# A three-stage float64 decode (two ReLUs and four VectorE operations) becomes a two-stage one (one parametric ReLU and two VectorE operations)

## The chip, the cores and the metric

The kernel runs on one core of one Trainium2 chip. The metric is device time in microseconds (us): median of 3 runs 1004.88 us (1004.45 to 1008.42). Five engines of the core work side by side, each through its own list of instructions in order: PE (TensorE: matmuls, with its weight loads PEld), DVE (VectorE), ACT (ScalarE), POOL (GpSimd) and SP (SyncE, which here issues every DMA). An instruction that waits for another engine holds up all that stands behind it in its own list.

## The reference

A linear attention with a decaying state (4 batches, 8 heads, 768 positions, head size 48), then two feed-forward layers over 3072 tokens of width 384:

```
cur   = outer(u * k_t, v_t)                      # per batch and head, 48 x 48
y_t   = r_t @ (state + cur)
state = w[:, None] * state + outer(k_t, v_t)
x = y as (batch, position, head * 48)
x = (sigmoid(x @ w_gate) * (x @ w_val)) @ w_out  # hidden width 1536
h = maximum(x @ w_in, 0)                         # hidden width 2048
out = (h * h) @ w_out2
```

The weights of both layers reach the device as 8-byte floats (their bytes are declared as int64); all products are float32 products.

## The kernel before, in words

The sequence is cut into 6 chunks of 128 positions; with 4 batches a chunk holds 512 tokens. An attention *unit* is one chunk of one batch (all eight heads). The hidden width of a layer is cut into blocks `f` of 128 columns (12 in layer 1, 16 in layer 2).

Every float32 matmul is made of three fp32r matmuls: both operands are split into a high and a low part, and high x high, low x high and high x low are added up in PSUM (`product`, `proj_out`). So one block `f` of layer 1 on 512 tokens is 9 matmuls for the gate (`pg`), 9 for the value (`pv`) and 9 for the output (`po`/`two`), each 128x128 by 128x512.

The work runs in *phases*. Phase 0 is layer 1 of chunk 0, blocks 0 to 6 only (`CUT` = 7); phases 1 to 5 are layer 1 of chunks 1 to 5, 12 blocks each; then chunk 0's other 5 blocks (`REDO`), and then layer 2 of all chunks. Ahead of phase 0 stands a start stretch with the four attention units of chunk 0. Beside the matmuls of phase `i` runs the attention of chunk `i + 1`: `unit_ops` spreads its steps over the phase's slots, three slots for each block, called by `fill(f, 0)`, `fill(f, 1)` and `fill(f, 2)` inside `inner`. There is no scheduler: the order of the code is the order on each engine.

A step `f` of layer 1 goes so: PE makes `pg`; ACT takes the sigmoid `s`; `fill(f, 0)`, which may hold a unit's matmuls into `ya` and `yb` (`attn_out`) and ACT's copies of them to `ys`; PE makes `pv` in the same PSUM buffer as `yb`, so after ACT's copy; DVE multiplies `pv` and `s`; ACT rounds the product to `gh`; `fill(f, 1)`; the rest `gl` = `s` - `gh` (on POOL in phase 0, on DVE later); PE adds the output product of the block before (`finish`); `fill(f, 2)`.

The weights lie in HBM in 68 *raw* pieces of 128 x 384 eight-byte numbers: for layer 1 gate, value and output of each block, so that block `f` needs pieces 3f, 3f+1 and 3f+2. Each piece is decoded once, by `convert()`, and stays in SBUF in two float32 parts, `wu`. The slots call `convert()`, at most once each (twice in the first slot of phase 0): about three pieces a block in phase 0, 15 pieces over phase 1, the 32 pieces of layer 2 during phase 5 and `REDO`.

The `n`-th call of `convert()` works on several pieces at once, in stages:

- piece n: two ReLUs on ACT (L146, L147) turn the low word into min(low / 2^29, 7), three bits
- piece n-1: DVE puts together the sign bit of the high word and those three bits in `wt_` (L159), and clears the sign in the top 16 bits (L167)
- piece n-2: DVE subtracts 16 * 896 from the top 16 bits and clamps at zero (L153), and puts the high word, shifted left by 3, into `wt_` (L163), which now holds float32
- piece n-3: ACT rounds `wt_` into the high part of `wu` (L132), POOL makes the low part (L133)

Four buffers hold raw pieces (`NRB`). Call `n` loads piece n+2, into the buffer of piece n-2, so SP waits for L163 there. Attention touches DVE too: `attn_mask` (L284, from PSUM), `attn_prep` (L232), `attn_sum` (L238, which gives `dv`), `attn_state` (L352, L353); ACT makes the diagonals `am` from `dv` (L248).

Of the kernel before, what the change touches and what calls it, by code (L numbers as in the profile page):

```python
# [7 lines left out]
F32 = mybir.dt.float32  # L8
F32R = mybir.dt.float32r
BF16 = mybir.dt.bfloat16  # L10
U8 = mybir.dt.uint8
I32 = mybir.dt.int32
U32 = mybir.dt.uint32
U16 = mybir.dt.uint16
I64 = mybir.dt.int64
AF = mybir.ActivationFunctionType
ALU = mybir.AluOpType
# [6 lines left out]
P = 128  # L24
DM = H * D
KT = DM // P
F1 = 12
# [14 lines left out]
def tile_kernel(  # L42
# [12 lines left out]
    nc = tc.nc  # L55
# [4 lines left out]
    sp = ctx.enter_context(tc.tile_pool(name="sp", bufs=2))  # L60
# [3 lines left out]
    NRB = 4  # L64
    NW = 36
    IN_W = 8
    CUT = 7
# [5 lines left out]
    seven = cp.tile([P, 1], F32, name="seven")  # L73
# [17 lines left out]
    def load_unit(n):  # L91

        if n >= NU:
            return
        c, b = units[n]
        got, o = [], 0
        for i, (tag, m, nb) in enumerate(PIECES):

            t = first[n][i] if n < IN_W else sp.tile([P, m], F32, tag=tag, name=tag, bufs=nb)
            got.append((t, rkv[c, b, :, o : o + m]))  # L100
            o += m
        for i in (2, 3, 0, 1):
            nc.sync.dma_start(out=got[i][0], in_=got[i][1])
        k_t[n], r_t[n] = (t[0:DP].rearrange("p (j t) -> p j t", j=HP) for t, _ in got[:2])
        kv_t[n], rn_t[n] = got[2][0], got[3][0]

    wunit = {}

    wqueue = [(w1[i, j], (1, i, j)) for i in range(F1) for j in range(3)]
    wqueue += [(w2[i, j], (2, i, j)) for i in range(F2) for j in range(2)]  # L110
    raws, parts, loaded = {}, {}, set()
    wn = [0]
    NWQ = len(wqueue)

    def load_raw(n):
        if n < NWQ and n not in loaded:
            loaded.add(n)
            raws[n] = sp.tile([P, KT * P], I64, tag="raw", name="raw", bufs=NRB)
            nc.sync.dma_start(out=raws[n], in_=wqueue[n][0])

    def convert():

        V = nc.vector
        n = wn[0]
        wn[0] += 1
        if n - 3 in parts:
            f1 = parts.pop(n - 3).bitcast(F32)  # L130
            w = wp.tile([P, 2, KT * P], F32R, tag="w", name="wu", bufs=NW)
            nc.scalar.copy(w[:, 0], f1)  # L132
            nc.gpsimd.tensor_tensor(out=w[:, 1], in0=f1, in1=w[:, 0].bitcast(F32), op=ALU.subtract)  # L133
            wunit[wqueue[n - 3][1]] = w

        def views(raw):
            two = [
                raw.bitcast(d).rearrange("p (n two) -> p n two", two=2) for d in (I32, F32, U32)
            ]
            top = raw.bitcast(U16).rearrange("p (n four) -> p n four", four=4)[:, :, 3]  # L140
            return [x[:, :, 0] for x in two] + [two[0][:, :, 1], top]

        if n < NWQ:

            lo, lof, lou, _, _ = views(raws[n])
            nc.scalar.activation(lof, lou, AF.Relu, bias=seven, scale=-(2.0**-29))  # L146
            nc.scalar.activation(lo, lof, AF.Relu, bias=seven, scale=-1.0)  # L147
        old, new = n - 2 in parts, 0 <= n - 1 < NWQ
        if old:

            raw, t = raws.pop(n - 2), parts[n - 2]
            _, _, _, hi, top = views(raw)
            V.tensor_scalar(  # L153
                out=top, in0=top, scalar1=16.0 * 896, scalar2=0.0, op0=ALU.subtract, op1=ALU.max
            )
        if new:
            lo, _, _, hi1, top1 = views(raws[n - 1])
            t1 = parts[n - 1] = sp.tile([P, KT * P], I32, tag="wt", name="wt_", bufs=3)
            V.scalar_tensor_tensor(  # L159
                out=t1, in0=hi1, scalar=-0x80000000, in1=lo, op0=ALU.bitwise_and, op1=ALU.bitwise_or  # L160
            )
        if old:
            V.scalar_tensor_tensor(  # L163
                out=t, in0=hi, scalar=3, in1=t, op0=ALU.logical_shift_left, op1=ALU.bitwise_or
            )
        if new:
            V.tensor_scalar(out=top1, in0=top1, scalar1=0x7FFF, scalar2=None, op0=ALU.bitwise_and)  # L167
        load_raw(n + NRB - 2)


    def tables():
# [49 lines left out]
    def attn_pre(n):  # L221
        if n >= NU:
            return
        rn = rn_t[n]
        side(n).tensor_tensor(out=rn, in0=rn, in1=kv_t[n][:, HD:], op=ALU.mult)
        side(n).tensor_tensor(out=rn, in0=rn, in1=u_bc, op=ALU.mult)

    def attn_prep(n):
        if n >= NU:
            return  # L230
        for t in (k_t[n], r_t[n]):
            nc.vector.tensor_mul(t, t, trk)  # L232

    def attn_sum(n):
        if n >= NU:
            return
        dv_t[n] = sp.tile([C, H], F32, tag="dv", name="dv", bufs=3)
        nc.vector.tensor_reduce(  # L238
            out=dv_t[n], in_=rn_t[n].rearrange("p (h d) -> p h d", d=D), axis=AX.X, op=ALU.add
        )  # L240
# [9 lines left out]
    def attn_kh(n):  # L250

        if n >= NU or units[n][0] == NCH - 1:
            return
        k = kv_t[n][:, HD:]
        side(n).tensor_tensor(out=k, in0=k, in1=th, op=ALU.mult)
# [285 lines left out]
    def warm(n):  # L541

        pw = pp.tile([P, T], F32, tag="g", name="pw") if n else None
        for _ in range(n):
            nc.tensor.matmul(pw, lhsT=idle[:, 0:P], rhs=idle, start=True, stop=True)

    with tc.manual_schedule():
        nc.vector.memset(idle, 0.0)
        warm(WARM0)
        nc.vector.memset(seven, 7.0)  # L550
        nc.scalar.activation(seven, seven, AF.Sigmoid)
        nc.vector.memset(seven, 7.0)
        nc.sync.dma_start(out=w_sb, in_=wt)
        id_sb = sp.tile([DP, D], F32, tag="ev", name="id_sb", bufs=2)
        maskf = sp.tile([C, C], F32, tag="ev", name="maskf", bufs=2)
        load_unit(0)
        nc.sync.dma_start(out=u_bc, in_=u.to_broadcast([C, H * D]))
        nc.sync.dma_start(out=anti, in_=antid)
        nc.sync.dma_start(out=maskf, in_=mask)
        nc.sync.dma_start(out=id_sb, in_=ident)  # L560
        load_unit(1)
        load_raw(0)
        load_raw(1)
        for n in range(2, B):
            load_unit(n)
            load_raw(n)
        powers = tables()
        attn_pre(0)
        nc.gpsimd.tensor_copy(mask8, maskf)
        attn_prep(0)  # L570
        attn_sum(0)
        attn_pre(1)
        attn_diag(0, 0)
        attn_diag(0, 1)
        attn_scores(0)
        attn_prep(1)
        attn_sum(1)
        state_tables(*powers)
        attn_mask(0)
        attn_diag(1, 0)  # L580
        attn_diag(1, 1)
        attn_kh(0)
        attn_kh(1)
        convert()
        for n in range(B):
            attn_scores(n + 1)
            attn_pre(n + 2)
            attn_prep(n + 2)
            warm(WARM_OUT[n])
            attn_out(n)  # L590
            attn_sum(n + 2)
            attn_mask(n + 1)
            attn_diag(n + 2, 0)
            attn_diag(n + 2, 1)
            attn_kh(n + 2)
            if n == 0:
                convert()
        for _ in range(2):
            convert()
        warm(WARM_X)  # L600
        for k in range(KT):
            x_from(0, k)
        for i, (layer, c, f0, f1) in enumerate(phases):
            ops = unit_ops(i + 1, f1 - f0) if i + 1 < NCH else []
            slot = 0

            def fill(f, j):

                nonlocal slot
                for op in ops[slot] if ops else []:  # L610
                    op()
                slot += 1
                lim = 0
                if i == 0:
                    lim = 3 * CUT + 3
                elif i == 1:
                    base = 3 * CUT + 3
                    lim = min(base + slot * (3 * F1 + 3 - base) // 27, 3 * F1 + 3)
                elif i == NCH - 1 and j < 2:
                    lim = min(3 * F1 + 3 * f - 1, 3 * F1 + 3 * CUT + 2)  # L620
                elif i == REDO and j < 2:
                    lim = 3 * F1 + 3 * f - 1
                elif i == REDO + 1 and j == 2:
                    lim = NWQ + 3
                for _ in range(2 if i == 0 and slot == 1 else 1):
                    if wn[0] < lim:
                        convert()

            for f in range(f0, f1):
                while (layer, f, 1) not in wunit:  # L630
                    convert()
                inner(i, f, fill)
        finish()
# [68 lines left out]
```

## Time and profile before

| | |
|---|---|
| median of 3 runs | 1004.88 us (1004.45 to 1008.42) |
| profiled execution, its own time | 1005.36 us |
| its span, first to last instruction | 1003.6 us (1.8 us lie around it) |
| mean granted TensorE clock | 0.985 of full |
| PE busy | 959.5 us, 96% |
| DVE busy | 544.6 us, 54% |
| ACT busy | 424.0 us, 42% |
| POOL busy | 133.9 us, 13% |

Busy shares are means over stretches that differ: after 216 us PE hardly rests and the others are half idle or more, in the first 220 us it is not so. A busy PE is also not PE at full speed: a matmul at the lower of the two clock levels is busy for twice as long. For the start, then, one goes stretch by stretch.

### The profile page before, as it was taken

The page shows a single profiled execution, that of the slowest core. Times are in us where ns is not written, and L with a number is a line of the kernel's source. Part 1 is how long each engine was busy: PE and PEld are TensorE (multiplying, and loading weights), DVE is VectorE, ACT ScalarE, POOL GpSimd, SP SyncE. Part 2 cuts the span into 40 slices and gives each one's busy share as a digit, 9 for nine tenths or more (in the row PEclk, how much of TensorE's full clock was granted, in tenths as well). Part 3 has the DMA queues.
Part 4 walks back from the last instruction along what each step waited for, and adds up shares of the span by engine and source line. Part 5 has one row for each costly group of instructions (what it writes and reads, how often), then busy time and mean ns, then how long its engine had stood idle before and what let it go on. Part 6 is the DMA issues. An engine that isn't in the chain of part 4 may idle for free.

```text
span 1003.6 us, 14066 instructions
## 1 busy us (share of the span) xinstructions
PE 959.5 (96%) x5544; PEld 760.7 (76%) x5544; DVE 544.6 (54%) x855; ACT 424.0 (42%) x870; POOL 133.9 (13%) x119
## 2 busy tenths in 40 slices
PE   7867798999999999999999999999999999999998
PEld 4555576778888888787888877888888888888886
DVE  7999978864444434431389787343433433433333
ACT  5766655643233323322377574232332322323322
POOL 6455643200000000000033132000000000000000
PEclk8989799999999999999999999999999999999999
DMA  9753544434122112200144440010010100100000
GB/s 316 245 179 101 154 130 129 131 106 132 52 60 73 61 52 59 89 7 15 63 125 124 160 148 27 1 63 0 1 64 1 47 17 1 63 1 1 32 1 31
DMA packets 42225, 76.75 MB, mean 76 GB/s; under 512 B 4912, under 2 KB 17584, under 8 KB 42160
## 3 DMA queue, kind: packets, MB, share of 16 engines
q1 hardware_dynamic: 42160, 75.87, 23.9%
q8 instruction: 43, 0.70, 0.3%
q14 instruction: 22, 0.18, 0.1%
HBM read 60.12 MB, written 11.01 MB: 71 GB/s over the span
## 4 chain that ended last, share of the span: by engine, by line
PE 80%; DVE 12%; DMA 3%; ACT 3%; issue 2%; SPq 1%; DVEq 0%; ACTq 0%
PE pg L384 31%; PE po L403 17%; PE two L403 14%; PE pv L384 12%; DVE raw L167 2%; DVE raw L153 2%; PE ya L298 2%; PE yb L298 1%; PE pa L266 1%; DVE am L284 1%; DMA raw<-in_w 1%; DVE first L232 1%; ACT am L248 1%; DVE s L527 1%; DMA first<-in_rkv 1%
## 5 line engine op out<-in xcount | busy, mean ns | idle before, releaser
L384 PE MATMUL pg<-xh,wu 128*128 128x512 f32 x1008 | 317.7, 400 | 11.7 <-ACT wu L132 7.5
L384 PEld LDWEIGHTS pg<-xh,wu 128*128 128x128 f32 x1008 | 191.2, 190 | 61.1 <-ACT wu L132 8.8
L531 ACT CAST gh<-s 128x512 fp32r<-128x512 f32 (+1 forms) x169 | 104.5, 618 | 219.4 <-DVE s L527 139.4
L384 PE MATMUL pg<-xl,wu 128*128 128x512 f32 x504 | 196.2, 397 | 0.0
L403 PE MATMUL po<-gh,wu 128*128 128x512 f32 (+1 forms) x542 | 169.0, 393 | 0.1
L530 DVE TENSOR_TENSOR s<-s 128x512 f32<-128x512 f32 (+1 forms) x97 | 66.7, 688 | 176.3 <-ACT s L529 176.3
L367 DVE TENSOR_TENSOR gl<-s,gh 128x512 fp32r<-128x512 f32 x162 | 113.1, 698 | 86.3 <-PE po L403 53.6
L384 PE MATMUL pv<-xh,wu 128*128 128x512 f32 x432 | 141.2, 408 | 15.8 <-ACT ys L336 11.3
L403 PE MATMUL two<-gh,wu 128*128 128x512 f32 x472 | 148.5, 395 | 0.0
L529 ACT ACTIVATE s<-pg 128x512 f32<-128x512 f32 (+1 forms) x97 | 57.5, 593 | 185.3 <-PE pg L384 185.3
L527 DVE TENSOR_TENSOR s<-pv,s 128x512 f32<-128x512 f32 x72 | 49.9, 692 | 150.4 <-PE pv L384 148.5
L403 PEld LDWEIGHTS po<-gh,wu 128*128 128x128 f32 x542 | 101.4, 188 | 24.6 <-ACT x2s L491 0.5
L384 PEld LDWEIGHTS pg<-xl,wu 128*128 128x128 f32 x504 | 95.6, 190 | 23.0 <-DVE xl L367 0.4
L384 PEld LDWEIGHTS pv<-xh,wu 128*128 128x128 f32 x432 | 80.4, 190 | 39.8 <-ACT ys L336 14.5
L403 PE MATMUL po<-gl,wu 128*128 128x512 f32 (+1 forms) x271 | 106.5, 393 | 1.3 <-DVE gl L367 1.3
L403 PEld LDWEIGHTS two<-gh,wu 128*128 128x128 f32 x472 | 89.3, 190 | 21.3
L403 PE MATMUL two<-gl,wu 128*128 128x512 f32 x236 | 93.0, 394 | 1.8 <-DVE gl L367 1.8
L384 PE MATMUL pv<-xl,wu 128*128 128x512 f32 x216 | 86.1, 399 | 0.0
L513 ACT ACTIVATE s<-pg 128x512 f32<-128x512 f32 x72 | 42.8, 595 | 101.8 <-PE pg L384 101.7
L248 ACT ACTIVATE am<-anti,dv 128x128 f32<-128x128 f32 x192 | 60.5, 391 | 19.7 <-DVE dv L238 19.7
L403 PEld LDWEIGHTS po<-gl,wu 128*128 128x128 f32 x271 | 50.8, 187 | 13.5 <-DVE gl L367 2.3
L167 DVE TENSOR_SCALAR raw<-raw 128x384 uint16<-128x384 uint16 x68 | 55.5, 816 | 0.0
(366 smaller groups left out, 967.0 us busy)
## 6 DMA issues: line engine op xcount, KB each, us to landing
raw<-in_w SPq DMA_DIRECT2D x68, 384.0 KB, 3.1
kv<-in_rkv SPq DMA_DIRECT2D x16, 384.0 KB, 3.2
xin<-x2d SPq DMA_DIRECT2D x6, 768.0 KB, 4.3
out<-x2s SPq DMA_DIRECT2D x18, 256.0 KB, 2.0
first<-in_rkv SPq DMA_DIRECT2D x16, 256.0 KB, 5.7
kT<-in_rkv SPq DMA_DIRECT2D x16, 256.0 KB, 4.7
rT<-in_rkv SPq DMA_DIRECT2D x16, 256.0 KB, 5.1
x2d<-x2s SPq DMA_DIRECT2D x15, 256.0 KB, 2.0
```

Source lines behind the costliest of these rows:

```text
L153: V.tensor_scalar(out=top, in0=top, scalar1=16.0 * 896, scalar2=0.0, op0=ALU.subtract, op1=ALU.max)
L167: V.tensor_scalar(out=top1, in0=top1, scalar1=0x7FFF, scalar2=None, op0=ALU.bitwise_and)
L248: nc.scalar.mul(am_t[n][:, h], anti, dv_t[n][:, h : h + 1])
L298: nc.tensor.matmul(out[64 * q : 64 * q + m], lhsT=lhsT, rhs=rhs, start=(bk, q) not in opened, stop=True, skip_group_check=True,)
L367: (eng or nc.vector).tensor_tensor(out=dst, in0=src, in1=high.bitcast(F32), op=ALU.subtract)
L384: nc.tensor.matmul(ps, lhsT=a, rhs=b_, start=(i == 0), stop=(i == len(pairs) - 1))
L403: nc.tensor.matmul(po[k][:, ts], lhsT=a, rhs=b_[:, ts], start=(first and m == 0), stop=(last and m == 2 and ts is cuts[-1]),)
L513: nc.scalar.activation(s, pg, AF.Sigmoid)
L527: nc.vector.tensor_tensor(out=s[:, ts], in0=pv[:, ts], in1=s[:, ts], op=ALU.mult)
L529: nc.scalar.activation(s[:, ts], pg[:, ts], AF.Relu)
L530: nc.vector.tensor_mul(s[:, ts], s[:, ts], s[:, ts])
L531: nc.scalar.copy(gh[:, ts], s[:, ts])
```

## The change

The three pieces of arithmetic are arranged anew. The top 16 bits of an eight-byte number are sign, 11 bits of exponent and 4 of mantissa; read as bfloat16 (sign, 8 and 7 bits) their exponent field holds the upper 8 bits of the long exponent. One parametric ReLU on ACT multiplies this bfloat16 by 2^-112 where it is positive, and by 2^-112 * 2^32 where it is negative: that rebases the exponent, and sets for a negative number the bit that the shift by 3 then brings to the sign's place. The three low bits come from one DVE operation (multiply, min), and one more DVE operation shifts and joins. Stages per call: piece n: ACT's parametric ReLU and DVE's low bits; piece n-1: DVE's shift and join; piece n-2: ACT's rounding and POOL's rest. The whole is one call shorter, and the bounds of the slots (`lim`) are lowered by one. Call `n` loads piece n+3, into the buffer of piece n-1.

```
@@ convert()
-        if n - 3 in parts:
-            f1 = parts.pop(n - 3).bitcast(F32)
+        if n - 2 in parts:
+            f1 = parts.pop(n - 2).bitcast(F32)
             w = wp.tile([P, 2, KT * P], F32R, tag="w", name="wu", bufs=NW)
             nc.scalar.copy(w[:, 0], f1)
             nc.gpsimd.tensor_tensor(out=w[:, 1], in0=f1, in1=w[:, 0].bitcast(F32), op=ALU.subtract)
...
+            top = raw.bitcast(BF16).rearrange("p (n four) -> p n four", four=4)[:, :, 3]
...
+        if n - 1 in raws:
+            lo, _, hi, _ = views(raws.pop(n - 1))
+            t = parts[n - 1] = sp.tile([P, KT * P], I32, tag="wt", name="wt_", bufs=3)
+            V.scalar_tensor_tensor(
+                out=t, in0=hi, scalar=3, in1=lo, op0=ALU.logical_shift_left, op1=ALU.bitwise_or
+            )
         if n < NWQ:
-            lo, lof, lou, _, _ = views(raws[n])
-            nc.scalar.activation(lof, lou, AF.Relu, bias=seven, scale=-(2.0**-29))
-            nc.scalar.activation(lo, lof, AF.Relu, bias=seven, scale=-1.0)
-        old, new = n - 2 in parts, 0 <= n - 1 < NWQ
-        if old:
-            raw, t = raws.pop(n - 2), parts[n - 2]
-            _, _, _, hi, top = views(raw)
+            lo, lou, _, top = views(raws[n])
+            nc.scalar.activation(top, top, AF.Prelu, scale=2.0**-112, alpha=2.0**32)
             V.tensor_scalar(
-                out=top, in0=top, scalar1=16.0 * 896, scalar2=0.0, op0=ALU.subtract, op1=ALU.max
+                out=lo, in0=lou, scalar1=2.0**-29, scalar2=7.0, op0=ALU.mult, op1=ALU.min
             )
-        if new:
-            lo, _, _, hi1, top1 = views(raws[n - 1])
-            t1 = parts[n - 1] = sp.tile([P, KT * P], I32, tag="wt", name="wt_", bufs=3)
-            V.scalar_tensor_tensor(
-                out=t1, in0=hi1, scalar=-0x80000000, in1=lo, op0=ALU.bitwise_and, op1=ALU.bitwise_or
-            )
-        if old:
-            V.scalar_tensor_tensor(
-                out=t, in0=hi, scalar=3, in1=t, op0=ALU.logical_shift_left, op1=ALU.bitwise_or
-            )
-        if new:
-            V.tensor_scalar(out=top1, in0=top1, scalar1=0x7FFF, scalar2=None, op0=ALU.bitwise_and)
-        load_raw(n + NRB - 2)
+        load_raw(n + NRB - 1)
@@ slots: 3 * CUT + 3 becomes 3 * CUT + 2, and so on
```

The first place is DVE in block 0 of phase 0, from the state update to the product `s`; `raw` and `wt_` belong to the decode. Before:

```order
L353 TENSOR_TENSOR state<-state,us 112x192
L153 TENSOR_SCALAR raw<-raw 128x384
L159 SCALAR_TENSOR_TENSOR wt__693<-raw 128x384
L163 SCALAR_TENSOR_TENSOR wt__604<-raw,wt__604 128x384
L167 TENSOR_SCALAR raw<-raw 128x384
L153 TENSOR_SCALAR raw<-raw 128x384
L159 SCALAR_TENSOR_TENSOR wt__705<-raw 128x384
L163 SCALAR_TENSOR_TENSOR wt__693<-raw,wt__693 128x384
L167 TENSOR_SCALAR raw<-raw 128x384
L527 TENSOR_TENSOR s<-pv,s 128x512
```

The same place on DVE now (line numbers are those of the changed kernel, 10 lower outside the decode):

```order
L343 TENSOR_TENSOR state<-state,us 112x192
L145 SCALAR_TENSOR_TENSOR wt__675<-raw 128x384
L155 TENSOR_SCALAR raw<-raw 128x384
L145 SCALAR_TENSOR_TENSOR wt__684<-raw 128x384
L155 TENSOR_SCALAR raw<-raw 128x384
L517 TENSOR_TENSOR s<-pv,s 128x512
```

Eight decode operations stood between the state update and `s`; four stand there now, and the join (L145) comes ahead of the low bits (L155).

The second place is ACT from block 0 to block 1 of phase 0, after `gh`: the diagonals `am`, the decode, the sigmoid, and the copies `us` and `ys` out of `yb` and `ya`. Before:

```order
L248 ACTIVATE am<-anti,dv 128x128 x4
L132 CAST wu<-wt__693 128x384
L146 ACTIVATE raw<-raw,seven 128x384
L147 ACTIVATE raw<-raw,seven 128x384
L248 ACTIVATE am<-anti,dv 128x128 x4
L132 CAST wu<-wt__705 128x384
L146 ACTIVATE raw<-raw,seven 128x384
L147 ACTIVATE raw<-raw,seven 128x384
L513 ACTIVATE s<-pg 128x512
L334 COPY us<-yb 112x192
L336 COPY ys<-yb 112x2x128
L337 COPY ys<-ya 112x2x128
```

The same place on ACT now:

```order
L238 ACTIVATE am<-anti,dv 128x128 x4
L132 CAST wu<-wt__684 128x384
L153 ACTIVATE raw<-raw 128x384
L238 ACTIVATE am<-anti,dv 128x128 x4
L132 CAST wu<-wt__716 128x384
L153 ACTIVATE raw<-raw 128x384
L503 ACTIVATE s<-pg 128x512
L324 COPY us<-yb 112x192
L326 COPY ys<-yb 112x2x128
L327 COPY ys<-ya 112x2x128
```

One ACTIVATE stands where two stood; the diagonals, the sigmoid and the copies keep their places.

The third place is SP's queue in the start stretch, at the first unit's `xr` transfers. Before:

```order
L339 DMA xr<-ys 48x3x128
L340 DMA xr<-ys 48x3x128
L103 DMA first<-in_rkv 128x768
L103 DMA first<-in_rkv 128x384
L103 DMA first<-in_rkv 128x512 x2
```

The same place in SP's queue now:

```order
L329 DMA xr<-ys 48x3x128
L330 DMA xr<-ys 48x3x128
L119 DMA raw<-in_w 128x384
L103 DMA first<-in_rkv 128x768
L103 DMA first<-in_rkv 128x384
L103 DMA first<-in_rkv 128x512 x2
```

The load of raw piece 4 moved from after the start stretch to ahead of the attention inputs of the sixth unit. It is the only load whose place in the queue changed; PE's and POOL's orders are as before.

## Rows read from the trace of the kernel before

**Rows 1.** The page: chain that ended last, share of the span by engine

```profile
PE 80%; DVE 12%; DMA 3%; ACT 3%; issue 2%; SPq 1%; DVEq 0%; ACTq 0%
```

**Rows 2.** Windows: busy time of PE, PEld, DVE, ACT, POOL; granted clock, DMA share, GB/s

```profile
0.00:40.00 40.00, 30.03 (x359) 17.56 (x359) 32.55 (x52) 25.16 (x74) 22.35 (x27) 0.91 0.88 291
40.00:130.00 90.00, 69.34 (x509) 52.21 (x509) 85.13 (x122) 55.73 (x123) 48.34 (x38) 0.87 0.50 152
130.00:216.00 86.00, 78.91 (x597) 61.51 (x598) 69.28 (x115) 48.09 (x108) 26.06 (x22) 1.00 0.46 140
475.00:625.00 150.00, 148.70 (x638) 119.20 (x637) 113.30 (x188) 85.89 (x155) 37.19 (x32) 1.00 0.34 108
```

**Rows 3.** Timeline of PE: first gate matmuls of phases 0, 1, 2 and 3

```profile
40.94 3.12 PE L384 MATMUL pg<-xh,wu 128*128 128x512 f32 x6 [2.46 <-ACT xh L371]
...
127.85 1.56 PE L384 MATMUL pg<-xh,wu 128*128 128x512 f32 x6
...
225.15 1.56 PE L384 MATMUL pg<-xh,wu 128*128 128x512 f32 x6
...
313.04 1.56 PE L384 MATMUL pg<-xh,wu 128*128 128x512 f32 x6
```

**Rows 4.** Chain in order of time, phase 2: start, us, what

```profile
250.41 2.10 PE pg L384 x9
...
256.69 2.10 PE pg L384 x9
```

**Rows 5.** Waits of PE, 41 to 128 us: total us, times, longest

```profile
PE pv L384 <- ACT ys L336: 9.2, 2, 5.3
PE pg L384 <- ACT wu L132: 7.5, 3, 2.7
...
PE pg L384 <- POOL wu L133: 1.7, 3, 0.8
PE pv L384 <- POOL wu L133: 1.0, 1, 1.0
```

**Rows 6.** Waits of PE, 128 to 225 us

```profile
PE pv L384 <- DVE s L527: 3.5, 3, 1.2
PE two L403 <- DVE gl L367: 1.8, 3, 0.8
PE pv L384 <- ACT ys L336: 1.6, 1, 1.6
```

**Rows 7.** Waits of PE, 225 us to the end

```profile
PE po L403 <- DVE gl L367: 1.3, 1, 1.3
PE pv L384 <- ACT ys L336: 0.5, 1, 0.5
```

**Rows 8.** Windows of 5 us around the longest of these waits, columns as above

```profile
105.00:110.00 5.00, 5.00 (x15) 3.90 (x14) 4.86 (x8) 0.91 (x2) 1.86 (x2) 0.58 0.99 301
110.00:115.00 5.00, 5.00 (x23) 3.91 (x22) 5.00 (x8) 3.52 (x7) 4.79 (x3) 1.00 0.48 149
```

**Rows 9.** Windows of the instructions on raw pieces alone: DVE busy

```profile
40.00:130.00 90.00, 59.53 (x81) 0.87 0.50 152
130.00:216.00 86.00, 35.99 (x60) 1.00 0.46 140
```

**Rows 10.** Timeline of DVE, one decode call with POOL idle

```profile
92.01 0.60 DVE L153 TENSOR_SCALAR raw<-raw 128x384 uint16<-128x384 uint16 x1
92.40 0.59 DVE L159 SCALAR_TENSOR_TENSOR wt__1060<-raw 128x384 int32<-128x384 int32 x1
92.91 0.54 DVE L163 SCALAR_TENSOR_TENSOR wt__981<-raw,wt__981 128x384 int32<-128x384 int32 x1
...
94.00 0.69 DVE L527 TENSOR_TENSOR s<-pv,s 128x512 f32<-128x512 f32 x1
```

**Rows 11.** Timelines of DVE and POOL, start of a decode call beside POOL

```profile
59.22 1.35 DVE L153 TENSOR_SCALAR raw<-raw 128x384 uint16<-128x384 uint16 x1
...
59.11 1.00 POOL L133 TENSOR_TENSOR wu<-wt__693,wu 128x384 fp32r<-128x384 f32 x1 [5.58 <-ACT wu L132]
```

**Rows 12.** ACT's decode instructions: ns min/median/max, first and last start

```profile
L146 ACT ACTIVATE raw<-raw,seven x68: 634/651/682, 16.5 to 609.1; 128x384 f32<-128x384 uint32 x68
...
L132 ACT CAST wu<-wt__331 x1: 497/497/497, 37.5 to 37.5; 128x384 fp32r<-128x384 f32 x1
```

**Rows 13.** The page's DMA issues: KB each, us to landing

```profile
raw<-in_w SPq DMA_DIRECT2D x68, 384.0 KB, 3.1
```

**Rows 14.** Timelines of the start stretch: ACT's table load, DVE, ACT

```profile
0.73 1.28 ACT L551 ACT_TABLE_LOAD   x1 [0.73 <-PEq L691]
...
16.47 2.33 DVE L232 TENSOR_TENSOR first<-first,trk 112x512 f32<-112x512 f32 x2 [1.03 <-DMA first<-in_rkv]
...
40.27 1.66 ACT L371 CAST xh<-xr 128x512 fp32r<-128x512 f32 x3 [1.00 <-DMA xr<-ys]
```

More of the change, by code (lines that the diff above doesn't have):

```diff
@@ L133, in convert @@
             nc.gpsimd.tensor_tensor(out=w[:, 1], in0=f1, in1=w[:, 0].bitcast(F32), op=ALU.subtract)
-            wunit[wqueue[n - 3][1]] = w
+            wunit[wqueue[n - 2][1]] = w
         def views(raw):
[L137 to L141, printed above, removed]
@@ L143, in convert @@
-        if n < NWQ:
-            lo, lof, lou, _, _ = views(raws[n])
-            nc.scalar.activation(lof, lou, AF.Relu, bias=seven, scale=-(2.0**-29))
-            nc.scalar.activation(lo, lof, AF.Relu, bias=seven, scale=-1.0)
-        old, new = n - 2 in parts, 0 <= n - 1 < NWQ
-        if old:
-            raw, t = raws.pop(n - 2), parts[n - 2]
-            _, _, _, hi, top = views(raw)
+            two = [raw.bitcast(d).rearrange("p (n two) -> p n two", two=2) for d in (I32, U32)]
+            top = raw.bitcast(BF16).rearrange("p (n four) -> p n four", four=4)[:, :, 3]
@@ new lines, in views @@
+            return two[0][:, :, 0], two[1][:, :, 0], two[0][:, :, 1], top
+        if n - 1 in raws:
[4 more added lines that the diff above has]
+            )
+        if n < NWQ:
+            lo, lou, _, top = views(raws[n])
+            nc.scalar.activation(top, top, AF.Prelu, scale=2.0**-112, alpha=2.0**32)
@@ L549, in tile_kernel @@
         warm(WARM0)
-        nc.vector.memset(seven, 7.0)
+        nc.vector.memset(seven, 0.0)
         nc.scalar.activation(seven, seven, AF.Sigmoid)
-        nc.vector.memset(seven, 7.0)
         nc.sync.dma_start(out=w_sb, in_=wt)
@@ L614, in fill @@
                 if i == 0:
-                    lim = 3 * CUT + 3
+                    lim = 3 * CUT + 2
                 elif i == 1:
-                    base = 3 * CUT + 3
-                    lim = min(base + slot * (3 * F1 + 3 - base) // 27, 3 * F1 + 3)
+                    base = 3 * CUT + 2
+                    lim = min(base + slot * (3 * F1 + 2 - base) // 27, 3 * F1 + 2)
                 elif i == NCH - 1 and j < 2:
-                    lim = min(3 * F1 + 3 * f - 1, 3 * F1 + 3 * CUT + 2)
+                    lim = min(3 * F1 + 3 * f - 2, 3 * F1 + 3 * CUT + 1)
                 elif i == REDO and j < 2:
-                    lim = 3 * F1 + 3 * f - 1
+                    lim = 3 * F1 + 3 * f - 2
                 elif i == REDO + 1 and j == 2:
-                    lim = NWQ + 3
+                    lim = NWQ + 2
                 for _ in range(2 if i == 0 and slot == 1 else 1):
```

## The prediction

> **What bounds the kernel now.** I read the chain that ended last first: PE carries 80% of it, DVE 12% [rows 1]. So the kernel is a matmul kernel with a stretch somewhere in which DVE decides. The windows say where: from 40 to 130 us PE is busy for 69 of 90 us, DVE for 85.1, and the granted clock is 0.87; from 130 to 216 us PE has 78.9 of 86 and DVE 69.3; from 475 to 625 us PE lacks only 1.3 of 150 [rows 2]. Elsewhere the change touches nothing: all decoding lies in these three stretches and the start.
>
> The first matmuls of the phases give the sizes. Phase 0 lasts from 40.94 to 127.85 us, 86.9 us; phase 1 to 225.15, 97.3 us; phase 2, which decodes nothing, to 313.04, 87.9 us [rows 3]. Phase 2 is the yardstick: 12 blocks and four attention units on a PE that hardly waits. A block without attention takes 256.69 - 250.41 = 6.28 us in it [rows 4], of which the output product is about a third, 2.1 us. Phase 0 has the same four units, five blocks less and one output product less (that of its last block falls into phase 1): 87.9 - 5 x 6.28 - 2.1 = 54.4 us if PE never had to wait. So phase 0 loses 32.5 us, and phase 1 9.4 us against phase 2.
>
> What the losses are: in phase 0 PE waits 9.2 us for ACT's copies `ys` (two waits, the value product needs the PSUM of `yb`), 7.5 us for ACT's weights, 1.7 + 1.0 us for POOL's [rows 5]: 19.4 us. The other 13 us are slow matmuls: behind the 5.3 us wait, from 105 to 110 us, PE is busy all the time at a granted clock of 0.58, so mostly at 1.2 GHz, and at 1.00, 2.4 GHz, from 110 us on [rows 8]. A wait is thus paid nearly twice. In phase 1 the waits are 3.5 us for `s` and 1.8 us for `gl`, both DVE's, and 1.6 us for `ys` [rows 6].
>
> ACT and POOL are named in phase 0, but ACT is busy for only 55.7 of 90 us there and POOL for 48 [rows 2]. They stand behind DVE: `gh` waits for `s`, the diagonals for `dv`, the roundings for `wt_`. DVE is the full one, with 59.5 of its 85.1 us in the decode [rows 9].
>
> **The change part by part.**
>
> *DVE.* Each call loses two of four operations. With POOL idle, the four take 94.00 - 92.01 = 1.99 us from start to start; one TENSOR_SCALAR and one SCALAR_TENSOR_TENSOR of them, 92.91 - 92.01 = 0.90 us [rows 10]. The new low-bits operation works on 4-byte numbers, not 2-byte ones as L153, but reads and writes every other word, with as many elements; no row shows it. Lower bound the 0.39 us that L153 takes to the next start, upper bound the 0.51 us of L159 [rows 10]; I take 0.39. The join has L159's operands in L163's operation, 0.5 us by either. So a call is 1.1 us shorter with POOL idle. Beside POOL it is different: L153 took 1.35 us when POOL had begun a weight 0.11 us before it [rows 11], twice the time at rest. Over phase 0, 20 calls took 59.5 us [rows 9], 19.7 us more than 20 x 1.99. Is that surcharge halved with the operations? POOL runs as many instructions as before, so I count it as unchanged: it falls on what DVE does instead. DVE saves 20 x 1.1 = 22 us in phase 0 (31 us if the surcharge halves), and 15 x 1.1 = 16 us in phase 1.
>
> *Phase 0.* DVE's 85 us become 63. That is still above PE's 54.4, so DVE would still pace it, but now with ACT close behind it. ACT's list between `gh` and `ys` is, in blocks with an attention unit: two rounds of diagonals, two conversions, the sigmoid, three copies. It shrinks by two ReLUs only, and the join now waits for a parametric ReLU that stands behind those diagonals, as L159 did for L147. I leave the two waits for `ys` at about 2 us each, with 1 us of slow matmuls behind each: 6 us on top of 63, so 69 us. Gain 18 us. Bounds: 10 us (only the weights' waits of 10.2 us go) and 32.5 us (PE never waits).
>
> *Phase 1.* DVE falls from 69 of 86 us to 53; the 5.3 us of waits for `s` and `gl` should vanish, since each came behind one or two decode calls, and some of the 1.6 us. Gain 6 us, bounds 2 and 9.4.
>
> *Phase 5 and REDO.* The only wait is 1.3 us for a `gl` [rows 7], in a stretch where DVE was busy for 113 of 150 us [rows 2]: gain 1.3, bounds 0 and 1.3.
>
> *ACT.* Two ReLUs of 0.65 us become one parametric ReLU. Its price: no row shows one. Below it lies the rounding cast on as many elements with 0.50 us [rows 12], above it both ReLUs together, 1.30 us (the function has two branches). I take 0.65: same engine, same number and stride of elements. By 1.30 ACT would gain nothing, and phase 0 would lose about 5 of the 18 us: 2 x 0.65 us at each of the two waits for `ys`, which stand behind two conversions, and 0.65 at each of the three for ACT's weights.
>
> The Trainium skill ("ScalarE: Activation LUTs", What ACT_TABLE_LOAD costs) says that an ACTIVATE costs 186 ns + 0.833 ns an element with immediate scale and bias, 93 ns more for a bias that is read from SBUF, whatever the function: an estimate of 0.51 us for the parametric ReLU and 0.60 us for the old ones. The trace has 0.65 us for the ReLUs with the bias `seven`, a little above the rule; by the rule the sum would be about 1 us better, so it doesn't move the forecast.
>
> *Start stretch.* The low-bits operation of piece 0 lands where DVE idles for 1.03 us ahead of 16.47 us [rows 14]; the pair in the next call replaces a pair there. The load of piece 4 now waits in SP's queue for the first join and stands ahead of the sixth unit's inputs: 393 KB at the stretch's 291 GB/s [rows 2] are 1.35 us of transfer. But PE's first gate matmul waits for `xh`, and that for the `xr` transfer, by 1.00 us [rows 14], not for those inputs. I take 0; bounds 0 and +1.5 us, the price if the cover is gone.
>
> *Queues later.* The join frees a raw buffer as the first DVE operation of a call, where before L163 came third, so SP is released earlier; a piece is used three calls after its load is issued instead of two. But DVE now reads the raw piece itself, in front of `s`: a late load stops DVE, and behind it `s`, `gh` and PE.
>
> Sum: 18 + 6 + 1.3 = 25.3 us. The profiled execution took 1005.36 us (span 1003.6), 0.5 us over the median of 1004.88: 1005.4 - 25.3 = 980.1 us.
>
> **The rivals.**
>
> *ScalarE takes VectorE's place.* For it: the longest waits are for `ys`, behind ACT's ordered list; and a faster DVE waits for the parametric ReLU at every join, as it did twice for L147. Against: ACT has 38% of phase 0 free. Then phase 0 gives about 11 us and phase 1 4: 990 us. A parametric ReLU of 1.3 us belongs here.
>
> *PE becomes the bound.* For it: the surcharge beside POOL halves too, DVE comes to 53 us in phase 0, below PE's 54.4, and once waits are short the slow clock goes with them. Then nearly all of 32.5 + 9.4 + 1.3 = 43.2 us return; with a tenth left, 966 us.
>
> *The function brings table loads.* The Trainium skill ("ScalarE activation tables: per-element evaluation and per-set limits", What a function is on this engine) says that functions of different sets are a table load of 1283 ns apart. The trace has one load, of 1.28 us, at the start [rows 14]. Were the parametric ReLU in another set than the sigmoid, each sigmoid among decode calls would bring two: 7 in phase 0, 9 in phase 1, in all 32 x 1.28 = 41 us of ACT. In phase 0 ACT would have 55.7 - 13 + 18 = 61 us, in a list that others wait for: phase 0 about 80 us, phase 1 2 us better: 995 us. Against it: ACT's order of the changed kernel holds one table load, at its head.
>
> *Slower: late raw pieces stop DVE.* A piece lands 3.1 us after its issue [rows 13], and SP issues in order, behind `xr` transfers that wait for ACT. Each call saves DVE 1.1 us, so it decides from a mean wait of 1.1 us at the low-bits operation. At 1.6 us, 35 calls would lose 17 us: 1022 us. Against: with calls 69 / 21 = 3.3 us apart, a lead of three calls is about 10 us, and the core's DMA is half idle in phase 0 [rows 2].
>
> **How the numbers follow.** Forecast, 972 to 986 us: 0.55. ScalarE: 0.20. PE: 0.15. Table loads: 0.03. Late pieces: 0.03. Gains that melt to within 0.5%, about 5 us, which is what a measurement of this kernel can tell from no change: 0.04. So faster 0.93, same 0.04, slower 0.03. The range leaves out the lower half of the PE case and the last three cases: 966 to 994 us.
>
> **What would show it.** Right: phase 0 near 69 us and phase 1 near 91; PE's waits for ACT's and POOL's weights gone, those for `ys` shorter; the granted clock near 1 in phase 0; a parametric ReLU near 0.65 us and DVE's pair at 0.9 us at rest. Wrong: a wait of DVE for the raw load or the parametric ReLU that adds up to more than 10 us, a phase 0 above 76 us or below 60, or a phase 0 that begins later than 42 us.

## The result and the profile after

The changed kernel took 979.53 us (median of 4, 979.15 to 980.53) against 1005.68 us (4 runs, 1004.45 to 1008.42): ratio 0.9738, 95% interval 0.9715 to 0.9761. Forecast: 980.0 us, 966 to 994. Its profiled execution took 980.53 us, with a span of 978.7.

The chain that ended last (the page's line by engine) answers to [rows 1]:

```profile
PE 88%; DVE 4%; ACT 3%; DMA 2%; issue 2%; POOL 1%; SPq 1%; DVEq 0%; ACTq 0%
```

DVE's share fell from 12 to 4%, PE's rose from 80 to 88%. PE's first gate matmuls of phases 0 to 3 answer to [rows 3]:

```profile
41.70 3.12 PE L374 MATMUL pg<-xh,wu 128*128 128x512 f32 x6 [3.86 <-ACT xh L361]
...
113.82 1.56 PE L374 MATMUL pg<-xh,wu 128*128 128x512 f32 x6
...
202.10 1.56 PE L374 MATMUL pg<-xh,wu 128*128 128x512 f32 x6
...
289.99 1.56 PE L374 MATMUL pg<-xh,wu 128*128 128x512 f32 x6
```

So the time came back like this:

| stretch | before | after | difference | forecast |
|---|---|---|---|---|
| start to phase 0 | 40.94 | 41.70 | +0.8 | 0 |
| phase 0 | 86.9 | 72.1 | -14.8 | -18 |
| phase 1 | 97.3 | 88.3 | -9.0 | -6 |
| phase 2 | 87.9 | 87.9 | 0.0 | 0 |
| phase 3 to the end | 690.6 | 688.7 | -1.9 | -1.3 |
| span | 1003.6 | 978.7 | -24.9 | -25.3 |

The windows of phases 0 and 1 (busy PE, PEld, DVE, ACT, POOL; granted clock, DMA share, GB/s), which answer to [rows 2], here cut at the phases' own ends:

```profile
41.70:113.80 72.10, 61.41 (x500) 46.59 (x501) 54.23 (x76) 47.58 (x100) 43.54 (x35) 0.93 0.60 183
113.80:202.10 88.30, 88.01 (x645) 70.88 (x644) 59.52 (x96) 49.30 (x104) 25.28 (x22) 1.00 0.45 137
```

DVE is busy for 54 of 72 us in phase 0; before it was full. In phase 1 PE lacks 0.3 us. PE's waits from 41 to 114 us, against [rows 5]:

```profile
PE pv L374 <- ACT ys L326: 4.4, 2, 2.5
PE pg L374 <- ACT xh L361: 3.9, 1, 3.9
PE pg L374 <- ACT wu L132: 3.0, 3, 1.2
PE pg L374 <- POOL wu L133: 2.7, 4, 0.8
PE pv L374 <- POOL wu L133: 0.6, 1, 0.6
```

The waits for `ys` and for ACT's weights are halved and more; those for POOL's weights are no shorter (2.7 and 0.6 us, before 1.7 and 1.0). The 3.9 us for `xh` lie ahead of phase 0's first matmul. So in phase 0 PE waits 10.7 us (72.1 - 61.4), where it waited 19.7 (86.9 less 67.2 busy); and its busy time fell from 67.2 to 61.4 us for the same matmuls. After 114 us only this is left, so the waits of [rows 6] for `s` and `gl` and the one of [rows 7] for `gl` are gone:

```profile
PE pv L374 <- ACT ys L326: 0.8, 2, 0.5
```

The granted clock in windows of 5 us, against [rows 8]:

```profile
45.00:50.00 5.00, 5.00 (x84) 3.96 (x82) 0.00 (x0) 1.39 (x5) 0.00 (x0) 0.69 0.87 328
50.00:55.00 5.00, 3.00 (x12) 1.94 (x12) 4.61 (x9) 2.96 (x5) 2.23 (x2) 0.99 0.31 76
55.00:60.00 5.00, 5.00 (x44) 3.62 (x47) 3.10 (x6) 3.23 (x8) 0.85 (x1) 0.66 0.53 184
...
65.00:70.00 5.00, 5.00 (x23) 3.99 (x23) 4.87 (x8) 2.69 (x5) 3.92 (x5) 1.00 0.97 302
```

Two stretches at the lower level are left in phase 0, both in its first 20 us; from 60 us on no window of 5 us is below 1.00, though PE waits there too, by at most 2.5 us at once.

Now the decode itself. ACT's and DVE's new operations (ns min/median/max, first and last start), against [rows 12]:

```profile
L153 ACT ACTIVATE raw<-raw x68: 1049/1083/1117, 17.0 to 587.6; 128x384 bf16<-128x384 bf16 x68
...
L155 DVE TENSOR_SCALAR raw<-raw x68: 342/355/1461, 16.0 to 589.2; 128x384 int32<-128x384 uint32 x68
```

The parametric ReLU takes 1.08 us, not 0.65; the low bits take 0.355 us at rest. ACT begins its next instruction 0.81 us after the start of the parametric ReLU (58.98 to 59.79 us), where the two ReLUs took 1.23 us together (58.94 to 60.17 us): ACT's list is 0.42 us a call shorter. A call that waits for ACT beside a busy POOL, and a call at rest (POOL idle), to the start of the next instruction, against [rows 11, 10]:

```profile
60.13 1.68 DVE L145 SCALAR_TENSOR_TENSOR wt__731<-raw 128x384 int32<-128x384 int32 x1 [2.04 <-ACT raw L153]
61.74 1.15 DVE L155 TENSOR_SCALAR raw<-raw 128x384 int32<-128x384 uint32 x1
...
577.13 0.56 DVE L145 SCALAR_TENSOR_TENSOR wt__5353<-raw 128x384 int32<-128x384 int32 x1
577.60 0.36 DVE L155 TENSOR_SCALAR raw<-raw 128x384 int32<-128x384 uint32 x1
577.87 0.69 DVE L520 TENSOR_TENSOR s<-s 128x512 f32<-128x512 f32 x1
```

At rest a call takes 577.87 - 577.13 = 0.74 us, where four operations took 1.99. The decode's whole share of DVE in phase 0, against [rows 9]:

```profile
40.00:112.00 72.00, 27.33 (x38) 0.93 0.59 180
```

19 calls (38 operations) take 27.3 us, 1.44 us a call; before it was 59.5 / 20 = 2.98 us. And DVE waits for what it did not wait for much before (its waits from 41 to 114 us):

```profile
DVE wt__936 L145 <- ACT raw L153: 2.2, 1, 2.2
DVE wt__1275 L145 <- ACT raw L153: 2.1, 1, 2.1
DVE wt__1068 L145 <- ACT raw L153: 2.1, 1, 2.1
DVE wt__731 L145 <- ACT raw L153: 2.0, 1, 2.0
DVE wt__916 L145 <- ACT raw L153: 1.1, 1, 1.1
DVE wt__1255 L145 <- ACT raw L153: 1.1, 1, 1.1
```

Six joins wait 10.6 us for the parametric ReLU.

### The profile page after: what moved, and what is told of

The parts are those of the page before. It is cut to its first block, busy times and chain, and to the rows that moved or that the text cites. A ratio compares the mean times of both kernels' runs of the same rounds, so it can differ in the third digit from the quotient of the medians.

```text
span 978.7 us, 13895 instructions
## 1 busy us (share of the span) xinstructions
PE 952.3 (97%) x5544; PEld 758.0 (77%) x5544; DVE 454.4 (46%) x718; ACT 406.9 (42%) x802; POOL 128.5 (13%) x119
## 4 chain that ended last, share of the span: by engine, by line
PE 88%; DVE 4%; ACT 3%; DMA 2%; issue 2%; POOL 1%; SPq 1%; DVEq 0%; ACTq 0%
PE pg L374 35%; PE po L393 19%; PE two L393 16%; PE pv L374 14%; PE ya L288 2%; PE yb L288 2%; DMA first<-in_rkv 1%; PE pa L256 1%; ACT am L238 1%; DVE first L222 1%; DVE raw L155 1%; ACT raw L153 1%; DVE am L274 1%; POOL wu L133 1%; ACT wu L132 0%
## 5 line engine op out<-in xcount | busy, mean ns | idle before, releaser
L374 PE MATMUL pv<-xh,wu 128*128 128x512 f32 x432 | 138.4, 401 | 5.7 <-ACT ys L326 5.2
L153 ACT ACTIVATE raw<-raw 128x384 bf16<-128x384 bf16 x68 | 73.5, 1081 | 0.0
```

The lines of the kernel that those rows point to most:

```text
L153: nc.scalar.activation(top, top, AF.Prelu, scale=2.0**-112, alpha=2.0**32)
L374: nc.tensor.matmul(ps, lhsT=a, rhs=b_, start=(i == 0), stop=(i == len(pairs) - 1))
```

## The experiments

**Theory**: the gain is the two VectorE operations, and what is left in phase 0 is ACT's ordered list. **Rivals**: the gain comes from the ReLU saved on ACT, from the shorter pipeline or the earlier loads; or what is left is GpSimd's contention. All times are medians; the kernel before ran beside each at 1005.65 to 1006.06 us.

| run | edit | us | ratio to before (95%) |
|---|---|---|---|
| e1 | + two DVE operations a call | 1007.44 | 1.0011 (1.0001 to 1.0021) |
| e2 | + one ReLU on ACT a call | 985.53 | 0.9787 (0.9772 to 0.9802) |
| e3 | plain ReLU | 980.00 | 0.9732 (0.9716 to 0.9748) |
| e4 | before, one ReLU less | 1001.45 | 0.9961 (0.9948 to 0.9974) |
| e5 | before, two DVE operations less | 987.59 | 0.9805 (0.9790 to 0.9820) |
| e6 | loads one call later | 978.43 | 0.9730 (0.9717 to 0.9744) |
| e7 | decode ahead of attention | 982.82 | 0.9768 (0.9751 to 0.9786) |
| e8 | weights' rest on DVE | 988.95 | 0.9844 (0.9818 to 0.9870) |
| e9 | parametric ReLU on float32 | 978.02 | 0.9721 (0.9704 to 0.9739) |
| e10 | e9 and e6 | 977.07 | 0.9722 (0.9709 to 0.9736) |
| e11 | the changed kernel again | 980.45 | 0.9747 (0.9730 to 0.9763) |
| e12 | e10 again | 976.21 | 0.9706 (0.9686 to 0.9726) |

**e1: the two VectorE operations back, on scratch.**

```
+            V.tensor_scalar(out=stop, in0=stop, scalar1=0x7FFF, scalar2=None, op0=ALU.bitwise_and)
+            V.scalar_tensor_tensor(
+                out=scr2, in0=shi, scalar=3, in1=slo, op0=ALU.logical_shift_left, op1=ALU.bitwise_or
+            )
```

> The changed kernel with two more VectorE operations per decode call, of the two kinds that were removed, on a scratch tile that nobody else reads. Theory (the gain is VectorE's two operations): VectorE in phase 0 goes from 50 of 70 us busy back above 70, phase 0 from 72 to 80-87 us, phase 1 from 88 to 92-96 us, total 991-1003 us. Rival (the gain is the ReLU saved on ScalarE and the shorter pipeline, VectorE's work hides): below 985 us.

1007.44 us: all of the gain is gone, and more than the theory's range. PE's first gate matmuls of phases 0, 1 and 2, and the window of phase 0:

```profile
46.31 2.24 PE L382 MATMUL pg<-xh,wu 128*128 128x512 f32 x6 [3.10 <-ACT xh L369]
...
133.16 1.56 PE L382 MATMUL pg<-xh,wu 128*128 128x512 f32 x6
...
227.91 1.56 PE L382 MATMUL pg<-xh,wu 128*128 128x512 f32 x6
...
46.30:133.20 86.90, 66.13 (x501) 49.85 (x502) 77.07 (x117) 47.70 (x100) 40.33 (x35) 0.86 0.47 149
```

PE's two largest sums of waits in that window:

```profile
PE pv L382 <- ACT ys L334: 9.1, 2, 4.6
PE pg L382 <- ACT wu L134: 8.6, 3, 3.7
```

Phase 0 has the 86.9 us of the kernel before, and its waits (9.2 and 7.5 us in [rows 5]); phase 1 has 94.8. Another 4.6 us are in the start stretch, which I had left out of the expectation: the two extra operations come in its first two calls, and DVE's next attention operation behind them begins at 26.24 us instead of 23.95; the rest of the 4.6 us is not traced. The saved ReLU, the shorter pipeline and the earlier loads are all still there: with DVE's two operations back they give nothing in phase 0, and 2.5 us in phase 1.

**e5 and e4: each part alone, on the kernel before.** e5 leaves out L153 and L163, e4 puts one ReLU for two:

```
-            V.tensor_scalar(
-                out=top, in0=top, scalar1=16.0 * 896, scalar2=0.0, op0=ALU.subtract, op1=ALU.max
-            )
...
-            V.scalar_tensor_tensor(
-                out=t, in0=hi, scalar=3, in1=t, op0=ALU.logical_shift_left, op1=ALU.bitwise_or
-            )
```

```
-            nc.scalar.activation(lof, lou, AF.Relu, bias=seven, scale=-(2.0**-29))
-            nc.scalar.activation(lo, lof, AF.Relu, bias=seven, scale=-1.0)
+            nc.scalar.activation(lo, lou, AF.Relu, bias=seven, scale=-(2.0**-29))
```

> The kernel before with two of its four VectorE operations per decode call left out (L153 and L163; the weights are then not the reference's), ScalarE's two ReLUs, the three stages and the loads as before: VectorE's part of the change alone. Theory: 976-985 us, within 5 us of the whole change. Rival (ScalarE's saving or the earlier loads carry the gain): above 992 us.

> The kernel before with one of ScalarE's two ReLUs per decode call left out (the low bits are then wrong), VectorE's four operations as before: ScalarE's part of the change alone. Theory (VectorE paces first, ScalarE's list only behind it): 1000-1005 us. Rival (the two parts add up; the whole change gave 26 us and VectorE's part alone 18): 996-999 us.

e5 gives 18.5 us of the 26, 2.6 us outside the theory's range but far from the rival's; e4 gives 4.2, as the theory said. PE's first gate matmuls of phases 0, 1 and 2 in e5:

```profile
41.41 3.11 PE L377 MATMUL pg<-xh,wu 128*128 128x512 f32 x6 [1.92 <-ACT xh L364]
...
120.06 1.56 PE L377 MATMUL pg<-xh,wu 128*128 128x512 f32 x6
...
210.04 1.56 PE L377 MATMUL pg<-xh,wu 128*128 128x512 f32 x6
```

Phase 0 takes 78.7 us in e5 and phase 1 90.0: 8.3 of the 14.8 us of phase 0 and 7.3 of the 9.0 of phase 1. PE's waits from 41 to 130 us, first e5 and then e4, show what each clears:

```profile
PE pv L377 <- ACT ys L329: 10.8, 3, 5.3
PE pg L377 <- POOL wu L133: 2.3, 3, 1.2
PE pg L377 <- ACT xh L364: 1.9, 1, 1.9
PE pg L377 <- ACT wu L132: 1.0, 2, 0.7
```

```profile
PE pv L383 <- ACT ys L335: 6.5, 2, 4.0
PE pg L383 <- ACT wu L132: 6.0, 3, 3.6
...
PE pv L383 <- ACT wu L132: 1.5, 1, 1.5
```

Less work on DVE clears the waits for ACT's weights (7.5 us before, 1.0 now). In the kernel before, ACT's last wait ahead of each of those three roundings was for DVE: once for the join and twice, at the diagonals that stand ahead of the rounding, for `dv`:

```profile
51.72 0.51 ACT L132 CAST wu<-wt__604 128x384 fp32r<-128x384 f32 x1 [2.13 <-DVE wt__604 L163]
...
78.60 1.28 ACT L248 ACTIVATE am<-anti,dv 128x128 f32<-128x128 f32 x4 [4.11 <-DVE dv L238]
...
117.63 1.28 ACT L248 ACTIVATE am<-anti,dv 128x128 f32<-128x128 f32 x4 [3.66 <-DVE dv L238]
```

It leaves the waits for `ys` (9.2 us before, 10.8). Less work on ACT shortens the waits for `ys` (6.5) and leaves the weights (6.0 + 1.5). So the two lists hold up different waits.

The two runs do not split the change into its parts. A call of e5 takes 0.98 us of DVE at rest (489.19 to 490.17 us), more than the change's 0.74, and e4 shortens ACT's list by 0.69 us a call, more than the change's 0.42. What gave the other 6.5 us of phase 0 is open: no run adds ACT's part to e5, or shortens the pipeline alone.

**e2: one more ReLU on ACT.**

```
+            nc.scalar.activation(sf, su, AF.Relu, bias=seven, scale=-(2.0**-29))
```

> The changed kernel with one more ScalarE ReLU per decode call, on a scratch tile. Theory (what is left of phase 0's loss is ScalarE's ordered list): 21 x 0.68 us more in that list in phase 0, of which half or more shows, phase 0 79-86 us, total 986-994 us. Rival (VectorE or GpSimd paces what is left, ScalarE has slack): at most 982 us.

985.53 us: 6.0 us slower than the changed kernel, between the two expectations and just below the theory's. The window of phase 0:

```profile
42.70:118.70 76.00, 64.75 (x500) 49.35 (x501) 51.31 (x76) 55.41 (x119) 42.66 (x35) 0.87 0.53 169
```

The expectation had the price wrong: 19 ReLUs are added there, of 0.61 us each, and ACT's busy time grows from 47.6 to 55.4 us, by 7.8. The phase grows by 3.9 us (42.75 to 118.72 us, against 72.1). Half of the added work shows, so ACT's list is a limit of phase 0, but not the only one.

**e3 and e9: why the parametric ReLU takes 1.08 us.** e3 changes the function, e9 the operand:

```
-            nc.scalar.activation(top, top, AF.Prelu, scale=2.0**-112, alpha=2.0**32)
+            nc.scalar.activation(top, top, AF.Relu, scale=2.0**-112)
```

```
-            top = raw.bitcast(BF16).rearrange("p (n four) -> p n four", four=4)[:, :, 3]
+            top = raw.bitcast(F32).rearrange("p (n two) -> p n two", two=2)[:, :, 1]
```

> The changed kernel with a plain ReLU (same scale, same bfloat16 operand in place) for the parametric one; negative weights become zero. If the parametric function costs the 0.43 us above a ReLU on 4-byte words: 0.65 us here, phase 0 66-69 us, total 973-977 us. If the operand does (2-byte elements, every fourth, in place): 1.08 us here too, total 979-980 us.

> The changed kernel with the parametric ReLU on the whole high word as float32 (the same sign and exponent bits, 23 instead of 7 below them; a power of two leaves them alone) instead of on its upper 16 bits as bfloat16. If the 2-byte operand costs the 0.43 us: the operation takes about 0.65 us, ScalarE's list in phase 0 is 9 us shorter, and by the price of e2 (6 us for 0.68 us a call) the total is 974-977 us. If the number of elements or the function costs it: 979-980 us.

The ACTIVATE in e3 and in e9:

```profile
L153 ACT ACTIVATE raw<-raw x68: 1043/1082/1097, 16.9 to 587.0; 128x384 bf16<-128x384 bf16 x68
```

```profile
L153 ACT ACTIVATE raw<-raw x68: 540/556/581, 16.8 to 585.7; 128x384 f32<-128x384 f32 x68
```

It is the operand: a plain ReLU on the same bfloat16 view takes 1.08 us too, and the parametric one on float32 words 0.556 us, half. But the kernel gained only 1.5 us by it (978.02 against 979.53, with ratios to before whose intervals overlap), where e2's price promised 4 to 5: my estimate was wrong. Phase 0 took 112.38 - 41.86 = 70.5 us, 1.6 less, where e3 and e11, with the order and the operands of the changed kernel, had 72.1 and 72.0. ACT is busy there for 39.8 us, 7.8 less than in the changed kernel: as much as e2 had added.

**e6, e10, e11, e12: the loads one call later, alone and with e9.**

```
-        load_raw(n + NRB - 1)
+        load_raw(n + NRB - 2)
```

> The changed kernel with each raw piece loaded one call later, as before the change (call n loads piece n+2), so that the load of piece 4 leaves its new place ahead of the sixth unit's inputs. Theory (the earlier load delays the xr transfers by 0.8 us and its lead is not needed): phase 0 begins near 41.0 instead of 41.7 us, total 978.5-979.3 us. Rival (a piece then comes too late and stops VectorE): 982 us or more.

> The later loads together with the parametric ReLU on the float32 word (e9). If the two small gains add: 976.5-977.5 us, the fastest so far. If the quicker decode needs the longer lead: 979 us or more.

> The changed kernel once more, beside e12 on the same chip: 978.5-980.5 us.

> The kernel of e10 once more, beside e11 on the same chip. If its gain over the changed kernel is real: 1.5-3.5 us below e11. If it was the spread between chips: within 1 us.

PE's first gate matmul in e6, whose wait for `xh` was 3.86 us in the changed kernel:

```profile
41.06 2.23 PE L374 MATMUL pg<-xh,wu 128*128 128x512 f32 x6 [0.85 <-ACT xh L361]
```

e6 comes out at 978.43 us (978.16 to 978.88), about 1 us better, and begins phase 0 at 41.06 us: the longer lead is not needed. The start varies by itself: phase 0 begins between 41.25 and 41.86 us in the changed kernel, e3, e7, e9 and e11, which load early, and between 40.40 and 41.06 in e6, e10 and e12, which load late. The two groups do not overlap and lie 0.9 us apart in the mean, so the load's place costs the start about what it had lost, though single executions spread by 0.6 us. Phase 0 of e6 is also shorter, 70.6 us, which I had not expected. Side by side on one chip e12 is 4.2 us faster than e11 (974.78 to 978.52 against 979.91 to 981.03), a little more than expected: it is the fastest version here, and faster than both kernels. In the profiled run of the same kernel in e10 phase 0 lasts 69.4 us:

```profile
40.50:109.90 69.40, 60.93 (x500) 45.70 (x501) 56.03 (x78) 39.46 (x100) 47.13 (x38) 0.95 0.60 191
```

ACT now has 39.5 us to do there, and still PE is busy for only 60.9 us.

**e7: decode ahead of attention in phase 0.**

```
+                todo = ops[slot] if ops else []
+                if i or j == 0:
+                    for op in todo: op()
+                    todo = []
...
+                for op in todo: op()          # after convert()
```

> The changed kernel with the decode call ahead of the attention steps, in the second and third slot of each block of phase 0. The parametric ReLU then stands ahead of the diagonals, so VectorE's join need not wait for those. Theory (that wait holds up phase 0): 974-977 us. Rival (the copies ys and the diagonals come later instead): 980-985 us.

982.82 us, the rival's. PE's longest wait from 41 to 116 us:

```profile
PE pv L374 <- ACT ys L326: 7.2, 2, 3.7
```

The joins wait 5.8 us for the parametric ReLU there instead of 10.6, but the diagonals come later on ACT (DVE now waits 4.6 us for them), and `ys` behind them: 7.2 us instead of 4.4. So this order loses more than it gains; what the joins' wait costs by itself it does not show.

**e8: the weights' rest on DVE instead of POOL.**

```
-            nc.gpsimd.tensor_tensor(out=w[:, 1], in0=f1, in1=w[:, 0].bitcast(F32), op=ALU.subtract)
+            nc.vector.tensor_tensor(out=w[:, 1], in0=f1, in1=w[:, 0].bitcast(F32), op=ALU.subtract)
```

> The changed kernel with the weights' low part made by VectorE instead of GpSimd: VectorE has one more operation of about 0.55 us per call, and GpSimd 1.0-2.2 us less per call, beside which VectorE's operations take twice as long. If that contention is what VectorE loses most by: phase 0 62-69 us, total 969-977 us. If the number of VectorE's operations decides: 982-990 us.

988.95 us, as the second expectation said, but not for its reason. DVE's longest wait from 40 to 116 us, and the window of phase 0:

```profile
DVE wu L133 <- ACT wu L132: 13.6, 12, 2.3
...
40.00:116.30 76.30, 62.80 (x501) 48.09 (x502) 54.98 (x98) 49.41 (x101) 19.01 (x16) 0.91 0.56 173
```

DVE does 22 operations more than the changed kernel (98 against 76) in 55.0 us busy, against 54.2. The decode's own 38 operations show why:

```profile
40.00:116.30 76.30, 18.81 (x38) 20.45 (x19) 0.91 0.56 173
```

They take 18.8 us instead of 27.3, with the same operands: 8.5 us less, without POOL's making of the rests beside them. What costs in e8 is a new wait: the rest needs ACT's rounding, and holds up DVE's list 12 times, 13.6 us. So the contention is real; what the changed kernel would gain without it, and without this wait, e8 does not show.

## Why the prediction was right, point by point

- *DVE bounds phase 0, and the two operations carry the gain*: right, with all of phase 0's gain gone in e1. e5 gives 18.5 of the 26 us alone, but only 8.3 of phase 0's 14.8.
- *The surcharge beside POOL stays, DVE comes to 63 us and still paces phase 0*: wrong. 19 calls took 27.3 us, 13.3 us over 19 x 0.74, where 19.7 had been over the rest time before: the surcharge fell by a third, with half the operations, and a call at rest costs 0.74 us, not 0.90. The 85 us that I started from also belong to the window of 90 us; in the phase itself DVE was busy for 82.9 of 86.9 us. It now has 54 us of work in 72.1 and idles for 18, so it does not pace the phase.
- *The parametric ReLU costs 0.65 us*: wrong, 1.08, inside the bounds of 0.50 and 1.30. e3 and e9 put it on the 2-byte operand; I had reckoned with the number of elements and the engine. Counted to the next start, ACT still saves 0.42 us a call, where I had 0.65. The estimate of 0.51 us from the Trainium skill ("ScalarE: Activation LUTs", What ACT_TABLE_LOAD costs) disagrees with this trace on the bfloat16 view, and comes near the 0.556 us of e9 on float32.
- *Phase 0 falls to 69 us, 63 of DVE and 6 of PE's waits for `ys` with slow matmuls behind them*: near, at 72.1 us, but it is not made up so. By the prediction's own 54.4 us for a PE that never waits it is 54.4 + 10.7 of waits + 7.0 of slower matmuls; before it was 54.4 + 19.7 + 12.8. The two waits for `ys` were 4.4 us, as estimated (2 each), but 3.0 us for ACT's weights and 3.3 for POOL's stayed, which I had let vanish; the granted clock was 0.93.
- *Phase 1 gains 6 us*: mis-sized by 3. It gained 9.0 of the 9.4 that were there to be had: PE's idle time there fell from 7.1 to 0.3 us, and its busy time from 90.2 to 88.0, a term that I had left out.
- *The waits in phase 5 and REDO*: the 1.3 us went; the rest of that stretch's 1.9 us is not assigned to a wait.
- *The start stretch costs nothing, 1.5 us if the cover is gone*: 0.8 us, about what the load's new place costs (e6, e10 and e12).
- *Late raw pieces stop DVE* and *table loads*: neither came; e6 shows that even the shorter lead is enough, and the changed kernel's trace has one table load, at 0.74 us.
- *ScalarE takes VectorE's place* (990 us): half true. ACT's list is a limit now (e2, and DVE's 10.6 us of waits, above the 10 us that I named as a sign against me), but a soft one.

The total came out within 0.5 us because phase 0's miss of 3.2 us and the start's 0.8 stand against phase 1's 3.0 and the last row's 0.6. What bounded phase 0 and what frees it was right; what paces it afterwards was wrong, and the closeness of the sum was luck.

Open: why phase 0 still takes 69.4 us in e10, against the 54.4 worked out for a PE that never waits. About 8 us are waits of PE, spread over ACT, POOL and, with 0.8 us, DVE; its busy time is 60.9 us, and the granted clock 0.95; which link of that ring to cut was not tried further.

## What to carry to other kernels

Where one engine is full and PE's waits carry other engines' names, follow those names back: the full engine's operations were what mattered, though PE waited for ACT. Once such an engine is relieved, its neighbours pace the stretch together, and the price of adding work there (3.9 us of phase 0 for 7.8 us of ACT's time) is not what taking as much away gives back (1.6 us). Put both parts' experiments beside each other: each of two lists may hold up waits of its own. And see that such an experiment takes away as much as the change does: e5 takes less of DVE's time, and e4 more of ACT's.

## What the runs showed of the hardware that I had not expected

- An ACTIVATE in place on 384 bfloat16 elements a partition, every fourth of the row, took 1.08 us, and the next ACTIVATE began 0.81 us after its start; on as many float32 elements, every other, 0.556 us, and 0.45 us to the next start. On the bfloat16 view the function (plain or parametric ReLU) made no difference.
- A TENSOR_SCALAR from uint32 to int32 on every other word took 0.355 us at rest, and the next instruction began 0.27 us after its start; on every fourth 2-byte element (uint16) it had taken 0.60 us.
- Moving POOL's 19 subtractions of phase 0 to DVE brought DVE's 38 decode operations there from 27.3 to 18.8 us, with operands unchanged.
